# Attention, then experts, then an MLP on one core: the second attention tile's scores in other PSUM banks with idle products behind them, and loads issued three at a time

## The chip, the cores and the metric

The kernel runs on one core of a Trainium2 chip. The metric is the device time of one execution in microseconds (us). Engines: TensorE (PE) multiplies matrices, VectorE (DVE) and ScalarE (ACT) do elementwise work, GpSimd (POOL) builds constants and issues indirect transfers, SyncE (SP) issues nearly all other transfers. PSUM is the memory that PE writes to, in banks of 512 fp32 columns; SBUF is the main on-chip memory.

## What is computed

Three layers, one after the other, on 1152 tokens (2 sequences of 576) with 512 features:

```python
# attention, 8 heads of 64, each query sees the 64 positions up to its own
scores = where(0 <= i - j < 64, q @ k.T / 8, -1e9)
x = softmax(scores) @ v                       # (1152, 512)
# each token goes to one of 8 experts, at most 288 tokens each
e = argmax(x @ w_gate); g = softmax(x @ w_gate)[e]
x = g * (relu(x @ w1[e]) @ w2[e])             # zero for tokens over the capacity
# MLP with a per-feature negative slope
h = x @ w_in                                  # (1152, 2048)
out = (max(h, 0) + alpha * min(h, 0)) @ w_out
```

## The kernel before, in words

The program is one straight list of instructions per engine; their order on each engine is the order in which the Python code emits them, and an engine takes its next instruction only when the one ahead of it has been taken. Semaphores carry the dependencies.

**Attention** (to about 41 us) goes through nine tiles of 128 tokens (`for t in range(NTILE + 2)`, lines 880 to 915). A tile is two chunks of 64 queries; a chunk sees two chunks of keys. The steps of one tile are spread over three rounds of the loop:

- `pe_scores(t)` (399): 16 products, which show as 32 matmuls, into two banks `sc`, one for each `s` (the first and second head of a pair); `p` counts the four pairs. The banks come from a pool of two, so the next tile's scores wait until both are read.
- `peak(t)` (412): DVE adds the mask and takes the row maximum, one instruction pair for each of the eight heads in the order `HEADS` (410), which alternates between the banks. Between heads, `step` lets DVE do a piece of the routing of earlier tiles, from the seventh tile on.
- `softmax(t)` (424): eight exponentials on ACT, in the same order.
- `pe_turn(t-1)`, `put_turn(t-1)` (429, 436): eight transposes of the earlier tile's exponentials, first bank's four heads first, then one copy for each bank from PSUM (ACT; for the last tile's second bank DVE).
- `pe_values(t-1)` (442): products with the values into a PSUM tile `av` of two banks, of which there is one; `put_values` (451) scales them on DVE into `xr`.
- `pe_columns`, `put_columns`, `pe_logits`, `put_logits` of `t-2` (461 to 479): transpose, copy, and gate logits.

**Inputs.** SP issues all queries (`qT`), keys (`kT`) and values (`v`) at the start in the order of their use (lines 272 to 291), 256 to 384 KB each; POOL copies values into a second, shifted layout (`more_values`, 326). `keep_busy(6)` (300, 306) puts six bf16 products of 512 columns on PE ahead of the first scores; their results are not used.

**The star.** After the first four tiles' routing, `choose_star` (629) picks the expert with the most tokens so far. SP reads its number and loads that expert's weights: four chunks of 512 KB by `load` (100) and four by `load_star_w2` (694), the latter into the room of the first sequence's keys and queries. POOL scatters the tokens' rows `xr` to HBM (`scatter`, 763) from the same time on. `go_ahead` (730) multiplies the star's weights with its first tokens while the last tiles are routed: line 745 reads the first four chunks, line 756 the other four. The next weights (`load_on(star_rows())`, 941) wait for rows that are gathered after all scatters.

**Experts** (to about 209 us) and **MLP** (to the end) split each fp32 weight into a high and a low part (ACT and DVE) and make three products for one; the change doesn't touch them.

Of the kernel before, what the change touches and what calls it, by code (L numbers as in the profile page):

```python
# [7 lines left out]
F32 = mybir.dt.float32  # L8
# [19 lines left out]
def attention_moe_mlp_kernel(  # L28
# [13 lines left out]
    nc = tc.nc  # L42
# [41 lines left out]
    at_expert = {}  # L84

    def moe_chunk(n):
        p, c = stream[n]
        if p not in at_expert:
            at_expert[p] = nc.values_load(inci[0:1, NS + p:NS + p + 1], engines=(mybir.EngineType.SP,),
                                          min_val=0, max_val=n_moe - 8)  # L90
        return wmoe[bass.ds(at_expert[p] + c, 1)].rearrange("o p f -> (o p) f")
# [8 lines left out]
    def take(n):  # L100
        slot = next(x for x in free if fits(n, x))
        free.remove(slot)
        place[n] = slot
        return slot

    def load(n, after=None):
        pool, tag = take(n)
        raws[n] = pool.tile([128, 1024], F32, name="raw", tag=tag)
        if n < n_moe:
            ins = nc.sync.dma_start(raws[n], moe_chunk(n))  # L110
            if after is not None:
                tc.add_manual_dep(ins.ins, after.ins.name, mybir.DependencyInfo(
                    mybir.DependencyClass.Sync, mybir.DependencyReason.DATA), reason="rows first")
        else:
            nc.sync.dma_start(raws[n].bitcast(I32), wmlp[n - n_moe].bitcast(I32))

# [105 lines left out]
    with tc.manual_schedule():  # L222
# [13 lines left out]
        with ExitStack() as es:  # L236
# [6 lines left out]
            ps_s = es.enter_context(tc.tile_pool(name="ps_s", bufs=2, space=PSUM))  # L243
            ps_t = es.enter_context(tc.tile_pool(name="ps_t", bufs=2, space=PSUM))
            ps_a = es.enter_context(tc.tile_pool(name="ps_a", bufs=1, space=PSUM))
            ps_l = es.enter_context(tc.tile_pool(name="ps_l", bufs=1, space=PSUM))

            kT, qT = ([pool.tile([128, NCH, 4, 64], F32, name=n, tag=n) for pool in heads_p] for n in ("kT", "qT"))
# [6 lines left out]
            lgs = att.tile([128, NTILE, NE], F32, name="lgs")  # L255
            xr = att.tile([128, NTILE, ROW], F32, name="xr")

            def load_heads(b, c0, c1):
                for dst, src in ((qT, q), (kT, k)):
                    nc.sync.dma_start(dst[b][:, c0:c1], src[b, :, c0:c1])  # L260

            def values(b, w):
                return vv[b][w % 2][w // 4][:, w // 2 % 2, :VW]

            def load_v(b, j):

                dst, n = (values(b, 2 * j), 128) if j < 4 else (values(b, 7)[64:], 64)
                nc.sync.dma_start(dst, v[b, 128 * j:128 * j + n, :])

            z = att.tile([128, 128], F32, name="z")  # L270
            nc.vector.memset(z, 0.0)
# [28 lines left out]
            def keep_busy(n):  # L300
                ps = ps_l.tile([128, 512], F32, name="idle", tag="lg")
                for _ in range(n):
                    nc.tensor.matmul(ps, busy[:, :128], busy, start=True, stop=True)
# [83 lines left out]
            def step(n=1):  # L387
                for _ in range(n):
                    if chain:
                        next(chain[0], None)  # L390
# [5 lines left out]
            def chunks(t):  # L396
                return [divmod(2 * t + e, NCH) for e in range(2)]

            def pe_scores(t):
                sc = [ps_s.tile([128, 4, 128], F32, name="sc", tag="sc") for _ in range(2)]  # L400
                for p in range(4):
                    for s in range(2):
                        h = slice(64 * s, 64 * s + 64)
                        for e, (b, i) in enumerate(chunks(t)):
                            w = max(i - 1, 0)
                            nc.tensor.matmul(sc[s][64 * e:64 * e + 64, p, :], qT[b][h, i, p, :],  # L406
                                             kT[b][h, w:w + 2, p, :])
                scs[t] = sc

            HEADS = [(p, s) for p in range(4) for s in range(2)]  # L410

            def peak(t, steps):
                nms[t] = sm.tile([128, 2, 4], F32, name="nm", tag="nm")
                sc = scs[t]
                scs[t] = [wk.tile([128, 4, 128], F32, name="ms", tag="ms") for _ in range(2)]
                pts[t] = [wk.tile([128, 4, 128], F32, name="pt", tag="pt") for _ in range(2)]
                m = mk[tuple(i == 0 for _, i in chunks(t))]
                for p, s in HEADS:
                    nc.vector.tensor_tensor_reduce(
                        out=scs[t][s][:, p, :], in0=sc[s][:, p, :], in1=m, scale=-0.125, scalar=3e38,  # L420
                        op0=ALU.add, op1=ALU.min, accum_out=nms[t][:, s, p:p + 1])
                    step(steps)
# [206 lines left out]
            def choose_star():  # L629
                key = once("skey", NE)  # L630
                most, keyp = once("most", 1), once("skeyp", 1, dtype=I32)
                nc.vector.tensor_tensor(key, so_far, rev, op=ALU.add)
                yield
                nc.vector.tensor_reduce(most, key, axis=AX.X, op=ALU.max)
                yield
                nc.vector.tensor_scalar(keyp, most, 64.0, None, op0=ALU.mult)
                yield
                nc.vector.tensor_scalar(star[:, 0:1], keyp, 56, 56, op0=ALU.bitwise_and, op1=ALU.bitwise_xor)
                yield
                at_expert[0] = nc.values_load(star[0:1, 0:1], engines=(mybir.EngineType.SP,),  # L640
                                              min_val=0, max_val=n_moe - 8)
                for c in range(4):
                    load(c)
                for n in range(2):
                    load_star_w2(n)
                nc.vector.tensor_scalar(bias, key, most, MARK, op0=ALU.is_equal, op1=ALU.mult)
                yield
                nc.vector.tensor_tensor(bias, bias, rev, op=ALU.add)
                yield
                mine = once("mine0", NE)  # L650
                nc.vector.scalar_tensor_tensor(mine, bias, MARK, found[:, 2], op0=ALU.is_ge, op1=ALU.mult)
                yield
                nc.vector.tensor_reduce(seg[:, 0:1], mine, axis=AX.X, op=ALU.add)
                yield
# [39 lines left out]
            def load_star_w2(n):  # L694

                two = heads_p[0].tile([128, 4 * S], F32, name=f"sw{n}", tag=("kT", "qT")[n])
                for c in (2 * n, 2 * n + 1):
                    w = two[:, 1024 * (c % 2):1024 * (c % 2) + 1024]
                    nc.sync.dma_start(w, wmoe[bass.ds(at_expert[0] + (4 + c), 1)].rearrange("o p f -> (o p) f"))
                    star_w2.append(w.rearrange("p (k f) -> p k f", k=2))  # L700
                    if c < 3:
                        raws[4 + c] = w
# [68 lines left out]
            def once(name, *shape, dtype=F32):  # L771
                return sm.tile([128, *shape], dtype, name=name, tag=name, bufs=1)
# [107 lines left out]
            for t in range(NTILE + 2):  # L880
                if t < NTILE:
                    pe_scores(t)
                    peak(t, 1 + (t in (6, 7)))
                if 1 <= t <= NTILE:
                    pe_turn(t - 1)
                    put_turn(t - 1)
                if t == NTILE:
                    run(*chain)
                    choose(b1)
                if t >= 2:  # L890
                    pe_columns(t - 2)
                    put_columns(t - 2)
                if t < NTILE:
                    softmax(t, HEADS)
                if t == NTILE + 1:
                    pe_ahead((0,))
                    dispatch(b1)
                    while waiting:
                        scatter(*waiting.pop(0))
                if 1 <= t <= NTILE:  # L900
                    pe_values(t - 1)
                if t >= 2:
                    pe_logits(t - 2)
                if 1 <= t <= NTILE:
                    put_values(t - 1)
                if t >= 2:
                    put_logits(t - 2)
                if t == NTILE:
                    pe_dispatch(b1)
                    weigh(b1)  # L910
                pe_free.append(t)
                step(2)
                pe_free.clear()
                if t == 5:
                    chain.append(route(b0))
# [452 lines left out]
        with tc.If(n_over > 0, preferred_fallthrough_block=True):  # L1368
# [31 lines left out]
            for p in range(NE):  # L1400
# [5 lines left out]
                with tc.If(here > 0), ExitStack() as es:  # L1406
# [6 lines left out]
                    at = nc.values_load(inci[0:1, NS + p:NS + p + 1], engines=(mybir.EngineType.SP,),  # L1413
                                        min_val=0, max_val=n_moe - 8)
# [84 lines left out]
```

## Time and profile before

| | us |
|---|---|
| three timed runs | 417.22, 417.91, 415.33 |
| their median | 417.22 |
| the profiled execution, its own time | 418.03 |
| its span, first to last instruction | 416.3 |

The profile is of one execution. A chain of waits is followed back from the last instruction: at each step to what released it, or to the instruction before it on its engine. A timeline row has the start, the duration (of a merged group from its first start to its last end), engine, line, operation, tile written and read, and in brackets the idle time before it with what ended it. In windows, PEclk is the granted clock of PE, 1.00 for 2.4 GHz and 0.50 for 1.2 GHz, and the DMA share is that of 16 transfer engines.

### The profile page before, as it was taken

How to read it: one execution, taken by the hardware profiler on the slowest of the kernel's cores; microseconds unless marked ns; L12 is line 12 of the kernel's file. 1: busy time of each engine (PE TensorE's matmuls, PEld its weight loads, DVE VectorE, ACT ScalarE, POOL GpSimd, SP SyncE). 2: the span in 40 equal slices, each digit the busy share in tenths (PEclk: the TensorE clock that was granted, in tenths of full speed). 3: DMA queues.
4: the chain of work that ended last, by engine and by line, in shares of the span. 5: the costliest groups of instructions: out<-in, count | busy, mean ns of one | idle time of the engine just before them, and what ended most of it. 6: DMA issues, size and time to landing. Idle time of an engine off the chain costs nothing.

```text
span 416.3 us, 7856 instructions
## 1 busy us (share of the span) xinstructions
PE 396.3 (95%) x2925; PEld 351.4 (84%) x2925; DVE 285.4 (69%) x676; ACT 198.2 (48%) x371; POOL 58.2 (14%) x125
## 2 busy tenths in 40 slices
PE   6999789999999998999999999999999999999990
PEld 4888588789999876779999988998899988999880
DVE  2788567688997854536779966999949982356220
ACT  3788415567376453333457655676307720255000
POOL 4721236310000560000000000000000000000431
PEclk9999869999999999999999999999999999999997
DMA  7920953999988899731423243333411000000221
GB/s 265 371 59 8 351 231 129 333 411 401 313 290 284 248 306 323 272 97 46 153 86 118 101 153 112 142 111 141 140 64 54 0 2 0 0 2 1 78 101 56
DMA packets 20447, 66.13 MB, mean 159 GB/s; under 512 B 2992, under 2 KB 2992, under 8 KB 20400
## 3 DMA queue, kind: packets, MB, share of 16 engines
q1 hardware_dynamic: 17872, 58.00, 39.9%
q0 software_dynamic: 2528, 7.53, 5.0%
q8 instruction: 25, 0.41, 0.4%
q14 instruction: 22, 0.18, 0.1%
HBM read 60.74 MB, written 4.79 MB: 157 GB/s over the span
## 4 chain that ended last, share of the span: by engine, by line
PE 87%; DVE 5%; DMA 3%; ACT 2%; issue 2%; POOLq 0%; ACTq 0%; POOL 0%; DVEq 0%
PE gps L220 24%; PE ops L1326 24%; PE y L220 8%; PE hps L1033 6%; PE sps L220 3%; PE sy L220 3%; DMA raw<-moe_in 3%; PE sc L406 3%; PE av L448 2%; PE tp L434 2%; PE py L1205 2%; PE aps L745 2%; PE ay L756 2%; PE tx L464 1%; PE xap L689 1%
## 5 line engine op out<-in xcount | busy, mean ns | idle before, releaser
L144 DVE TENSOR_TENSOR wlo<-raw,whi 128x1024 fp32r<-128x1024 f32 x45 | 54.2, 1223 | 19.2 <-ACT whi L1017 13.7
L220 PE MATMUL gps<-x2h,wlo 128*128 128x384 f32 x192 | 64.2, 334 | 0.0
L220 PE MATMUL gps<-x2h,whi 128*128 128x384 f32 x192 | 64.2, 334 | 0.0
L220 PE MATMUL gps<-x2l,whi 128*128 128x384 f32 x192 | 64.2, 334 | 0.0
L1326 PE MATMUL ops<-whi,gl 128*128 128x512 f32 x144 | 56.1, 390 | 0.0
L1326 PE MATMUL ops<-wlo,gh 128*128 128x512 f32 x144 | 56.1, 390 | 0.0
L1326 PE MATMUL ops<-whi,gh 128*128 128x512 f32 x144 | 56.0, 389 | 0.0
L1302 ACT ACTIVATE u<-gps,one 128x384 f32<-128x384 f32 x48 | 27.7, 577 | 55.0 <-PE gps L220 55.0
L1334 POOL DMA_INDIRECT out<-acc,tok x9 | 8.7, 965 | 245.9 <-ACTq L1368 233.1
L1303 DVE SCALAR_TENSOR_TENSOR g<-gps,slope,u 128x384 f32<-128x384 f32 x48 | 29.4, 613 | 18.9 <-ACT u L1302 18.8
L1332 DVE SCALAR_TENSOR_TENSOR acc<-ops,gate,acc 128x512 f32<-128x512 f32 x27 | 19.9, 748 | 30.7 <-PE ops L1326 30.7
L1017 ACT CAST whi<-raw 128x1024 fp32r<-128x1024 f32 x30 | 31.0, 1049 | 16.6 <-PE y L220 11.9
L220 PEld LDWEIGHTS gps<-x2l,whi 128*128 128x128 f32 x192 | 36.0, 188 | 0.1
L220 PEld LDWEIGHTS gps<-x2h,whi 128*128 128x128 f32 x192 | 36.0, 188 | 0.1
L220 PEld LDWEIGHTS gps<-x2h,wlo 128*128 128x128 f32 x192 | 36.0, 188 | 0.0
L1313 ACT ACTIVATE gh<-g,sign 128x384 fp32r<-128x384 f32 x48 | 29.3, 611 | 9.5 <-DVE g L1303 9.5
L1326 PEld LDWEIGHTS ops<-whi,gl 128*128 128x128 f32 x144 | 27.0, 188 | 5.6
L1326 PEld LDWEIGHTS ops<-wlo,gh 128*128 128x128 f32 x144 | 27.0, 188 | 5.6
L1326 PEld LDWEIGHTS ops<-whi,gh 128*128 128x128 f32 x144 | 27.0, 188 | 5.5
L1314 DVE SCALAR_TENSOR_TENSOR gl<-g,sign,gh 128x384 fp32r<-128x384 f32 x48 | 29.2, 609 | 0.2 <-ACT gh L1313 0.2
L220 PE MATMUL y<-hh,whi 128*128 128x256 f32 x96 | 27.7, 288 | 1.6 <-ACT spht L1196 1.6
L190 DVE TENSOR_TENSOR wlo<-w,whi 128x512 fp32r<-128x512 f32 x32 | 21.9, 686 | 7.9 <-ACT whi L189 7.8
(267 smaller groups left out, 816.5 us busy)
## 6 DMA issues: line engine op xcount, KB each, us to landing
raw<-moe_in SPq DMA_DIRECT2D x61, 512.0 KB, 4.9
raw<-mlp_in SPq DMA_DIRECT2D x32, 512.0 KB, 3.3
v<-v_in SPq DMA_DIRECT2D x8, 260.0 KB
sw<-moe_in SPq DMA_DIRECT2D x4, 512.0 KB, 11.4
qT<-q_in SPq DMA_DIRECT2D x6, 256.0 KB
kT<-k_in SPq DMA_DIRECT2D x6, 256.0 KB, 5.9
qT<-q_in SPq DMA_DIRECT2D x2, 384.0 KB
kT<-k_in SPq DMA_DIRECT2D x2, 384.0 KB, 5.5
```

The costliest lines, as they stand in the source:

```text
L144: eng.tensor_tensor(lo, raws.pop(split[c]), hi.bitcast(F32), op=ALU.subtract)
L190: nc.vector.tensor_tensor(lo, w, hi.bitcast(F32), op=ALU.subtract)
L220: nc.tensor.matmul(ps, wa[i], xa[j], start=start and n == 0, stop=stop and n == 2)
L406: nc.tensor.matmul(sc[s][64 * e:64 * e + 64, p, :], qT[b][h, i, p, :], kT[b][h, w:w + 2, p, :])
L1017: (nc.vector.tensor_copy if c % 4 == 3 else nc.scalar.copy)(ring_tiles(c)[0], raws[split[c]])
L1033: nc.tensor.matmul(ps[:, f, :], (hi, lo)[i][:, kk, fs], xt[j][:, kk, :], start=n == kk == 0, stop=n == 2 and kk == 3)
L1302: nc.scalar.activation(out=u, in_=ps, func=AF.Copy, scale=one[:, ft:ft + 1])
L1303: nc.vector.scalar_tensor_tensor(g, ps, slope[:, ft:ft + 1], u, op0=ALU.mult, op1=ALU.max)
L1313: nc.scalar.activation(out=gh, in_=g, func=AF.Copy, scale=sg)
L1314: nc.vector.scalar_tensor_tensor(gl, g, sg, gh.bitcast(F32), op0=ALU.mult, op1=ALU.subtract)
L1326: nc.tensor.matmul(ps, a_[:, ts_], b_[:, f % 2, :], start=f == 0 and n == 0, stop=f == 3 and n == 2)
L1332: nc.vector.scalar_tensor_tensor(acc[:, tt, :], ps, sc, acc[:, tt, :], op0=ALU.mult, op1=ALU.add)
```

## The change

Five edits.

1. The scores of the second tile (`t == 1`) are written to a tile `sc1` in the place of `av`, the two banks that hold the values' products, instead of the two `sc` banks.
2. Behind the scores of the first tile PE gets four idle products, behind those of the second tile three.
3. `HEADS` goes through the four pairs of the first bank, then those of the second.
4. Input transfers are counted in `paced`. From the ninth on each waits until the one three places ahead of it has landed. The first keys are issued on ACT's queue instead of SP's. The gate weights and `alpha` are not counted.
5. The star's eight weight loads are counted anew; from the fourth on each waits until the one three places ahead has landed.

```diff
 def load(n, after=None):
...
+            return ins
...
+            inputs = []
+            def paced(ins, n=8):
+                inputs.append(ins)
+                if len(inputs) > n:
+                    tc.add_manual_dep(ins.ins, inputs[-4].ins.name, mybir.DependencyInfo(
+                        mybir.DependencyClass.Sync, mybir.DependencyReason.DATA), reason="three at a time")
             def load_heads(b, c0, c1):
-                for dst, src in ((qT, q), (kT, k)):
-                    nc.sync.dma_start(dst[b][:, c0:c1], src[b, :, c0:c1])
+                for dst, src, queue in ((qT, q, nc.sync), (kT, k, nc.sync if b or c0 else nc.scalar)):
+                    paced(queue.dma_start(dst[b][:, c0:c1], src[b, :, c0:c1]))
...
             def load_v(b, j):
-                nc.sync.dma_start(dst, v[b, 128 * j:128 * j + n, :])
+                paced(nc.sync.dma_start(dst, v[b, 128 * j:128 * j + n, :]))
...
             def pe_scores(t):
-                sc = [ps_s.tile([128, 4, 128], F32, name="sc", tag="sc") for _ in range(2)]
+                if t == 1:
+                    both = ps_a.tile([128, 2, 512], F32, name="sc1", tag="av")
+                    sc = [both[:, s].rearrange("q (p k) -> q p k", k=128) for s in range(2)]
+                else:
+                    sc = [ps_s.tile([128, 4, 128], F32, name="sc", tag="sc") for _ in range(2)]
...
-            HEADS = [(p, s) for p in range(4) for s in range(2)]
+            HEADS = [(p, s) for s in range(2) for p in range(4)]
...
             def choose_star():
+                inputs.clear()
                 for c in range(4):
-                    load(c)
+                    paced(load(c), 3)
...
             def load_star_w2(n):
-                    nc.sync.dma_start(w, wmoe[bass.ds(at_expert[0] + (4 + c), 1)].rearrange("o p f -> (o p) f"))
+                    paced(nc.sync.dma_start(w, wmoe[bass.ds(at_expert[0] + (4 + c), 1)].rearrange("o p f -> (o p) f")), 3)
...
             for t in range(NTILE + 2):
                 if t < NTILE:
                     pe_scores(t)
+                    if t < 2:
+                        keep_busy(4 - t)
                     peak(t, 1 + (t in (6, 7)))
```

## Rows read from the trace of the kernel before

**Rows 1.** Page: PE's busy time and share; its clock in 40 slices.
```profile
PE 396.3 (95%) x2925; PEld 351.4 (84%) x2925; DVE 285.4 (69%) x676; ACT 198.2 (48%) x371; POOL 58.2 (14%) x125
...
PEclk9999869999999999999999999999999999999997
```

**Rows 2.** Chain of waits, first 20 us: start, us, what.
```profile
1.71 2.74 PE idle L303 x6
4.45 1.99 PE sc L406 x32
...
8.20 2.23 PE sc L406 x30
10.42 1.90 PE tp L434 x8
12.32 1.93 PE av L448 x32
14.25 1.03 PE sc L406 x32
...
16.75 1.08 PE av L448 x32
...
18.50 1.03 PE sc L406 x32
```

**Rows 3.** Timeline, first two tiles: exponentials, second scores, a copy.
```profile
6.86 2.44 ACT L426 ACTIVATE pt<-ms,nm 128x128 f32<-128x128 f32 x8 [4.56 <-DVE nm L419]
...
8.20 2.23 PE L406 MATMUL sc<-kT,qT 64*64 64x128 f32 x32 [1.83 <-DVE nm L419]
...
11.50 0.59 ACT L440 COPY ptT<-tp 128x512 f32<-128x512 f32 x1 [2.19 <-PE tp L434]
```

**Rows 4.** Windows: length, busy time of each engine, PEclk, DMA share, GB/s.
```profile
0.00:6.45 6.45, 4.66 (x38) 2.32 (x38) 0.79 (x4) 1.49 (x2) 2.46 (x12) 1.00 0.65 200
6.45:8.20 1.75, 0.01 (x1) 0.04 (x1) 1.68 (x15) 1.34 (x5) 0.57 (x2) 1.00 1.04 354
8.20:14.20 6.00, 6.00 (x75) 5.22 (x76) 1.88 (x18) 3.54 (x11) 5.41 (x40) 1.00 1.04 369
14.20:18.45 4.25, 4.21 (x97) 3.72 (x95) 3.95 (x23) 3.62 (x12) 2.94 (x9) 1.00 1.04 383
```

**Rows 5.** Issues of keys: count, size of one, median us to landing.
```profile
kT<-k_in SPq DMA_DIRECT2D x6, 256.0 KB, 5.9
```

**Rows 6.** Chain of waits, 40 to 64 us: start, us, what.
```profile
44.07 1.74 PE tx L464
...
47.40 2.04 ACT pt L426 x7
...
49.48 1.33 PE tp L434 x5
50.81 0.85 PE tx L464 x4
...
57.71 0.96 PE lg L474 x16
```

**Rows 7.** Timeline, ninth tile: VectorE and ScalarE after their waits.
```profile
45.75 0.29 DVE L419 CUSTOM_DVE_ANT_0 ms<-sc,mf 128x128 f32<-128x128 f32 x1 [3.15 <-PE tx L464]
45.83 1.07 ACT L440 COPY ptT<-tp 128x512 f32<-128x512 f32 x2 [4.43 <-PE tx L464]
```

**Rows 8.** Window of the lower granted clock, columns as in rows 4.
```profile
48.30:58.60 10.30, 9.76 (x93) 8.49 (x93) 6.01 (x35) 3.29 (x9) 1.11 (x3) 0.50 0.76 307
```

**Rows 9.** Transfer queues from 43 to 45 us: packets, MB, share.
```profile
q1 hardware_dynamic: 128, 0.46, 85.5%
```

**Rows 10.** Timeline and SP's waits: star's first loads, its first product, SP's next load.
```profile
41.22 2.42 SPq L110 DMA_DIRECT2D raw<-moe_in  x4
...
62.97 5.34 PE L745 MATMUL aps<-raw,axT 128*128 128x256 f32 x24
...
SPq L110 <- DMA sx<-xe,ixe: 24.1, 1, 24.1
```

## What is predicted, before the changed kernel is built or run

> **What bounds the kernel now.** I read the page first [rows 1]: TensorE (PE) is busy for 396.3 us, 95% of the span, so time can only be won where PE is idle, where it runs at the lower of its clock levels, or where it does work that can go. The row of slices shows the granted clock low in one place, in the slices after 40 us. Then I read the chain of waits of the first 20 us [rows 2] and of 40 to 60 us [rows 6]: the only two stretches that the edits touch.
>
> In the first stretch the reader is to see two things. The chain leaves PE once: the second tile's scores (8.20) wait for the last of eight peaks on VectorE (DVE), since both score banks are still being read; the timeline gives that wait as 1.83 us [rows 3]. And before 14.2 us everything on PE takes about twice as long as later: 32 score matmuls take 1.99 and 2.23 us, later 1.03; the values 1.93, then 1.08; the transposes in between took 1.90 [rows 2]. An idle product of 512 columns takes 2.74/6 = 0.46 us, which is the 1.2 GHz level. The column of granted clock reads 1.00 in these stretches [rows 4], so here I go by durations. PE worked from 1.71 to 6.44, was idle until 8.20, worked on without a gap, and was at 2.4 GHz from 14.2 on.
>
> In the second stretch one transpose stands in the chain for 1.74 us [rows 6], and VectorE and ScalarE (ACT) both wait for PE: 3.15 and 4.43 us that end at 45.8 [rows 7]. Afterwards the granted clock is 0.50 for 10.3 us [rows 8].
>
> The tiles between go at 4.25 us each with PE busy for 4.21 of them and VectorE for 3.95 [rows 4]. A lead won before them is carried through, as long as the inputs keep up.
>
> **The change, part by part.**
>
> 1. *Second tile's scores in the values' banks.* They no longer wait for the first tile's peaks: the 1.83 us go. In their place PE runs four idle products, then the scores, then three idle products. The values of the first tile now wait until the second tile's peaks have read those banks.
>
> When the clock rises with the gap filled I can't read anywhere, so I bound it. Earliest: everything from 6.45 on at 2.4 GHz. Four products 4 x 0.23 = 0.92 (half of the 0.46), scores 1.1 to 8.5, three products to 9.2. ACT's eight exponentials of the first tile end at 6.86 + 2.44 = 9.30 [rows 3], so the turn ends at 9.9 or so; two copies of 0.59 [rows 3], the values (1.1, half of them beside the second copy) end at 11.5. They end at 14.25 now [rows 2]: 2.7 won. Latest: the clock rises at 14.2 as now. Four products 1.83, scores 2.1, three products 1.37, turn 1.97, values 2.0: the values end near 15.7, 1.5 lost. Middle: it rises during the four products. They end at 7.8, the scores at 8.9, three products at 9.6, turn at 10.65, copies at 11.4, values at 12.0: 2.2 won. The second tile's peaks (1.76 us for eight, as now from 6.44 to 8.20, and from 8.9 on) end at 10.7, before the values want the banks at 10.9; that new wait is hidden by 0.2 us, and in the earliest case it is the limit. I take the middle, because PE then works without the 1.75 us of idleness that stood in its first 14 us.
>
> What is late next: VectorE. Between a tile's values and its logits it scales the values, takes the peaks of a later tile and copies the columns, nearly all of its 3.95 us for a tile [rows 4]. From 12.0 that gives logits at 15.85; they take 0.65 (from 16.75 + 1.08 to 18.50 [rows 2]), so the fourth tile's scores stand at 16.5, against 18.5 now. So **2.0 us** of the 2.2 are carried on; bounds 2.6 won and 1.5 lost.
>
> 2. *Order of heads.* Eight exponentials in the order of the banks instead of alternating. In the steady tiles PE reaches the turn after the exponentials are over, so nothing changes. For the last tile the chain shows five transposes behind the exponentials, 1.33 us, then the columns and the values [rows 6]. The seventh exponential ends at 49.44, the eighth near 49.75. With the first bank's four heads done halfway, one transpose is left behind the eighth, and the columns start at 50.1 instead of 50.8: 0.7 at the lower clock, half of that at the upper. I take **0.6**; bounds 0 (the bank's copy on ACT takes the place) and 0.9.
>
> 3. *Input transfers three at a time, from the ninth on; the first keys on ACT's queue.* The keys' issue now stands at the head of ACT's queue, whose first exponential is at 6.86 [rows 3]: hidden. The first scores start behind the idle products, so earlier keys win nothing. With the pacing, SP waits; behind it on its queue are only more inputs and, at 41 us, the star's weights. The cost is bandwidth. Now a key transfer of 256 KB takes 5.9 us from issue to landing [rows 5] at 383 GB/s [rows 4]: 2.26 MB, or 8.6 transfers, under way. What three give is not in the trace. Upper bound: the same 383 GB/s. Lower: in proportion, 3/8.6 of it, 134 GB/s. What is needed: the first eight transfers (2.1 MB) land near 8.6 (1.29 MB by 6.45, 0.62 more by 8.20 [rows 4]); then 2.24 MB more must be there for the fifth tile's scores at 18.5 + 4.25 - 2.0 = 20.7, that is 185 GB/s. In the first 6.45 us, in which transfers start one by one and the wait for the first bytes is included, 200 GB/s were moved [rows 4]. I take 300, between that row and the upper end, and the cost **0**.
>
> The Trainium skill (DMA: Bandwidth & Descriptors, "Anatomy of one DMA — SWDGE (gpsimd) path") gives a fixed 2.0 us beside the bytes at 436 GB/s, though for the other descriptor path. By that, an estimate: 256 KB take 2.6 us alone, and three under way move 0.30 MB per us. That is slower than the row but over the need, and it leaves the sum as it is.
>
> 4. *Star's weights three at a time.* The eight loads of 512 KB are issued from 41.22 on; the first product that reads them is at 62.97, and SP then waits 24.1 us for the star's gathered rows before its next load [rows 10]. All eight in the 21.7 us up to that product would be 193 GB/s, half of the 383 of rows 4, and the last four are wanted later still: hidden, cost 0. The weights that follow start when the star's rows are gathered, so I let their stream shift with the lead. Is there a gain? The stall at 42 to 46 lies exactly where loads and row scatters meet: in 43 to 45 us the load queue alone moved packets, 128 of them [rows 9]. If the deep load queue makes this stall, pacing shortens it. But VectorE's wait begins at 42.6 [rows 7], when at most three loads have been issued (four in 2.42 us from 41.22 [rows 10]), and three would still be under way. I take **0**; bounds: nothing, and 2.1 us of idleness plus the lower clock. The latter's worth: six PE pieces of the chain, from the transposes at 49.48 (1.33) to the logits at 57.71 (0.96), sum to 7.9 us at 0.50 [rows 6, 8]; at full clock about half, 3.7 us less.
>
> The Trainium skill (DMA: Bandwidth & Descriptors, "Queues, rings and completion order") says that each DMA engine goes round robin between the queues it has work for. By that rule a deep load queue could not hold the scatters back, pacing would change nothing here, and the first rival below would fall away. Rows 9, with one queue moving alone, show no such even sharing.
>
> Sum: 2.0 + 0.6 = 2.6 us. The profiled execution took 418.03 us, its span is 416.3, and the median of three runs is 417.22 (415.33 to 417.91): 0.8 lower, within their spread. 418.03 - 2.6 = 415.4 for an execution like it; 417.22 - 2.6 = **414.6** for the median.
>
> **Rivals.**
> - *The stall shrinks too.* For: its place, and that the load queue alone moves then. Against: it begins before a fourth load is issued. It would give the 2.6 plus 1.5 (some of the idleness) to 5.8 (all of it and the clock): 413.1 to 408.8, middle 410.5.
> - *The clock rises late.* Then the seven products lie on PE's path at 0.46 each and the first stretch loses 1.5 while the order of heads still wins 0.6: 417.22 + 0.9 = 418.1. For: 1.71 to 6.44 brought no rise. Against: the gap that followed is just what goes.
> - *Three transfers starve the attention (slower).* Place: the scores of the fifth tile and later. It decides from 185 GB/s downward. At 134 GB/s the remaining 5.0 MB last 37 us from 8.6, so the last tile's keys land at 46, where the loads of the star begin at 41.2 now, right beside that tile's scores: 4.7 later, 422. At 155 GB/s they land at 41: the gain is just eaten. Against: the 300 taken above. I put 420 on it.
>
> **How the numbers follow.** Forecast as summed 0.48; stall shrinks 0.27; late clock 0.13; starved 0.12. The forecast's own range is 413.5 to 416. With 418.5 at the top the late clock is in and only the starved runs are out; at the bottom 409 leaves out only the very best of the second case. One per cent, 4.2 us, is about what a measurement of this kernel tells from no change: faster by more (under 413.05) is 0.25 of the stall case and 0.09 of the forecast's early edge, 0.34; slower by more (over 421.4) is half of the starved case, 0.06; the rest, 0.60, is within it.
>
> **What would show it.** Right: in the changed profile the second tile's scores start near 7.8 without a wait on VectorE and last about 1.1; values of the first tile end near 12; the fourth tile's scores stand near 16.5; one transpose behind the last exponential; scores that wait for no input; star's first product about 2.6 us earlier than 62.97, with everything behind it shifted alike. Wrong: scores of 2 us after 8 us (late clock); scores waiting for a key transfer (starved); VectorE and ACT not waiting at the eighth tile, or no granted clock of 0.50 (the stall was the load queue's). If the lead is there at 17 us and gone at 170, it is lost in the weights' stream, and my claim that this shifts with the star's rows is the wrong step.

## The result: 413.51 us after, 417.37 before

20 runs of each kernel: before 417.37 us (414.86 to 418.89), after 413.51 (410.46 to 418.07), ratio 0.9911 [0.9892, 0.993]. That is 3.9 us less, 0.9%; the interval reaches from 2.9 to 4.5 us. The forecast was 414.6, the range 409.0 to 418.5. The profiled execution of after took 413.85 us, 4.2 less than that of before, and its span is 412.1, also 4.2 less. Here and below, ratios and intervals are taken from the fast runs of both kernels and are not the quotients of the medians beside them.

The page of after, lines that answer to [rows 1]:
```profile
PE 392.2 (95%) x2932; PEld 347.3 (84%) x2932; DVE 285.2 (69%) x676; ACT 198.2 (48%) x371; POOL 57.2 (14%) x125
...
PEclk9999899999999999999999999999999999999997
```
PE is busy for 4.1 us less though it has seven more instructions, and the fifth slice, which holds 41 to 51 us, reads 8 where before had 8 and 6 in two slices.

The timeline of after, first two tiles and then the ninth (start, duration, engine, line, operation, tiles, idle before), answering to [rows 3, 7, 10]. Line 420 is the scores, 313 the idle products, 448 the transposes, 462 the values, 433 the peaks, 454 the copies, 760 the star:
```profile
4.86 1.99 PE L420 MATMUL sc<-kT,qT 64*64 64x128 f32 x32 [0.41 <-DMA kT<-k_in]
6.77 1.14 PE L313 MATMUL idle<-ahead_y 128*128 128x512 bf16 x4
...
7.84 1.10 PE L420 MATMUL sc<-kT,qT 64*64 64x128 f32 x32
...
10.82 0.08 DVE L433 DVE_READ_ACCUMULATOR2_ANT nm<- 128x1 f32 x1
...
11.16 1.15 PE L462 MATMUL av<-v,ptT 128*64 128x65 f32 x32 [0.58 <-POOL back L360]
...
43.73 0.29 DVE L433 CUSTOM_DVE_ANT_0 ms<-sc,mf 128x128 f32<-128x128 f32 x1 [3.00 <-remote]
43.81 1.07 ACT L454 COPY ptT<-tp 128x512 f32<-128x512 f32 x2 [4.29 <-remote]
44.45 1.94 PE L462 MATMUL av<-v,ptT 128*64 128x65 f32 x32 [2.67 <-ACT ptT L454]
...
57.99 1.03 PE L760 MATMUL aps<-raw,axT 128*128 128x256 f32 x4
...
59.94 4.58 PE L760 MATMUL aps<-raw,axT 128*128 128x256 f32 x20 [0.93 <-issue]
```
The reader is to see three things. The second tile's scores start at 7.84 with no wait and take 1.10 where they took 2.23 from 8.20: the wait of [rows 3] is gone, and PE is on its upper level from about 7.0, when the four products (1.14 for four) speed up, instead of 14.2. (That part is not the edit alone: in all twelve profiles of the experiments below, two of them without edits 1 and 2, the clock first rose between 4.6 and 7.6 us. The profile of before is the only one in which it took until 14.2. The trace's record of the granted clock begins with the first rise; ahead of it the PEclk column of [rows 4] reads 1.00 without a record.) The values start at 11.16, 0.26 after the last peak of the second tile has ended at 10.90; the releaser in the brackets is inferred. (In a kernel of the third group that POOL instruction comes later than the values, and the values again start 0.26 after the last peak; in five kernels the profile names the last peak itself.) So the new wait on the banks is real, and is the last to end. At the ninth tile nothing has changed: VectorE and ScalarE still wait for 3.00 and 4.29 us, and PE for 2.67.

The chain of waits of after, first 20 us, then the last tile's turn, answering to [rows 2, 6]:
```profile
11.17 1.14 PE av L462 x32
...
15.92 0.64 PE lg L488 x16
16.56 1.03 PE sc L420 x32
...
46.39 0.76 PE lg L488 x16
47.15 1.45 PE tp L448 x8
```
The fourth tile's scores stand at 16.56, before at 18.50 [rows 2]: 1.94 us won between these two executions. How much of it is the late rise of the clock in the one of before is taken up below. The last tile's transposes (47.15) follow the logits at once, where five of them came behind the exponentials before [rows 6].

Windows of after, columns as in [rows 4]; the first two answer to those rows, the last two to [rows 8]:
```profile
8.20:14.20 6.00, 5.42 (x111) 4.48 (x104) 4.13 (x32) 5.22 (x17) 5.49 (x39) 1.00 0.74 246
14.20:18.45 4.25, 4.21 (x94) 3.71 (x93) 3.51 (x24) 3.41 (x11) 1.47 (x5) 1.00 0.86 286
44.45:47.98 3.53, 3.53 (x52) 3.51 (x53) 3.15 (x21) 3.25 (x10) 0.00 (x0) 0.52 1.03 390
47.98:52.00 4.02, 3.53 (x68) 3.14 (x67) 3.06 (x15) 1.28 (x3) 0.00 (x0) 1.00 0.89 348
```
With three transfers under way 246 to 286 GB/s are moved, where 369 and 383 were before, and nothing on PE waits for an input after the first scores. The low granted clock lasts 3.5 us here, 10.3 before [rows 8].

The ninth tile's values in the kernel before (timeline), for the line at 44.45 above:
```profile
46.47 1.17 PE L448 MATMUL av<-v,ptT 128*64 128x65 f32 x32 [2.13 <-ACT ptT L440]
```
Where the 4.2 us of the profiled pair come from: 1.94 at the fourth tile's scores; 2.0 at the ninth tile's values (44.45, before 46.47); 5.0 at the star's first product (57.99, before 62.97 [rows 10]), the extra 3.0 mainly, by its length, from the shorter stretch at the lower clock. Behind that product the changed kernel waits 0.93 us, which the kernel before did not, and 4.2 are left at the end. What this wait is was not found.

So far this reads like the prediction's step 1 with some luck. The experiments say otherwise.

### The profile page after: what moved, and what is told of

Its sections match the earlier page's. It is cut to its first block, busy times and chain, and to the rows that moved or that the text cites. A ratio compares the mean times of both kernels' runs of the same rounds, so it can differ in the third digit from the quotient of the medians.

```text
span 412.1 us, 7881 instructions
## 1 busy us (share of the span) xinstructions
PE 392.2 (95%) x2932; PEld 347.3 (84%) x2932; DVE 285.2 (69%) x676; ACT 198.2 (48%) x371; POOL 57.2 (14%) x125
## 4 chain that ended last, share of the span: by engine, by line
PE 84%; DMA 4%; DVE 3%; ACT 2%; issue 2%; another core or an unknown queue 1%; POOL 1%; SPq 0%; POOLq 0%; ACTq 0%
PE gps L221 24%; PE ops L1343 24%; PE y L221 8%; PE hps L1050 6%; PE sps L221 3%; PE sy L221 3%; DMA raw<-moe_in 3%; PE av L462 2%; PE py L1222 2%; PE aps L760 2%; PE ay L771 2%; PE sc L420 2%; PE tp L448 1%; DVE wlo L145 1%; DMA v<-v_in 1%
```

## The experiments

Kernels ran in three groups of four, each group on one chip beside the kernel before: 418.25 us (35 runs), 410.19 (28) and 417.06 (31). The chips differ by 2%, so ratios are compared, inside a group first; the changed kernel itself ran only in the third group and in the first comparison. Where the expectations use letters, A is the prediction's account, in which the pacing is worth nothing, and C the one on packets of instructions that is formed below.

### First group: are the parts worth what the prediction gave them?

**The change without pacing.** No transfer waits, and the first keys are on SP's queue again.
```diff
-                if len(inputs) > n:
+                if False:
-                for dst, src, queue in ((qT, q, nc.sync), (kT, k, nc.sync if b or c0 else nc.scalar)):
+                for dst, src, queue in ((qT, q, nc.sync), (kT, k, nc.sync)):
```


> The change without its transfers' pacing: all inputs and star loads issued as before, keys on SP's queue. Left in: scores of the second tile in the values' banks, idle products, order of heads. If pacing is worth nothing (theory A): the same as the whole change, 3.9 us below the kernel before, within 0.7; first scores back at 4.4 instead of 4.86. If pacing brings the part of the gain that the prediction didn't count (theory B): 2.6 us below before or less, so at least 1.3 slower than the whole change. The low clock after 44 us: under A its length varies as it likes, under B it is longer than the 3.4 us of the change.

Measured: 418.83 us, ratio 0.9994 [0.9956, 1.0032]. No gain is left. The front is as in the changed kernel (values at 11.20), and then PE stops twice with nothing in the profile that it waits for. Timeline of this kernel:
```profile
16.53 0.54 PE L420 MATMUL sc<-kT,qT 64*64 64x128 f32 x9
18.34 0.88 PE L420 MATMUL sc<-kT,qT 64*64 64x128 f32 x23 [1.27 <-issue]
...
24.33 0.27 PE L478 MATMUL tx<-identf,xr 128*128 128x128 f32 x1
25.59 0.55 PE L478 MATMUL tx<-identf,xr 128*128 128x128 f32 x3 [0.99 <-issue]
```
The stops lie inside a run of equal products, 9 into the fourth tile's scores and, a round later, 1 into the third tile's transposes for the gate: 1.27 + 0.99 = 2.26 us, which eats the lead of 1.9 to 2.0.

**Only the pacing.** The kernel before with both pacings and the first keys on ACT's queue; scores, products and order of heads are those of before.
```diff
-                if t == 1:
-                    both = ps_a.tile([128, 2, 512], F32, name="sc1", tag="av")
...
-            HEADS = [(p, s) for s in range(2) for p in range(4)]
+            HEADS = [(p, s) for p in range(4) for s in range(2)]
...
-                    if t < 2:
-                        keep_busy(4 - t)
```


> The kernel before with the pacing alone, and the first keys on ACT's queue. Theory A: no change, within 0.7 us, or 0.4 slower because the first keys land later. Theory B: 1.3 us or more below the kernel before, with a shorter stall at 42 to 46 us or a shorter stretch at the low clock. The fifth tile's scores wait for no input in either.

Measured: 417.33 us, ratio 0.9974 [0.9945, 1.0003]: between 2.3 us won and 0.1 lost, so neither nothing, as the prediction had it, nor 1.3 us is excluded. PE doesn't stop, and this execution had something to lose. The front is that of before, but PE's clock first rose at 5.73, fell at 9.15 behind the wait for the peaks and rose again at 12.56, where before it rose at 14.19. So this execution has a lead without edits 1 and 2, and keeps it. Chain of waits, fourth and sixth tile's scores, then the sixth tile's of before (the fourth tile's stand at 18.50 [rows 2]):
```profile
17.44 1.03 PE sc L416 x32
...
25.98 1.03 PE sc L416 x32
```
```profile
27.04 1.03 PE sc L406 x32
```
1.06 us ahead at both places.

**Banks and products alone** (edits 1 and 2): as the first kernel, and `HEADS` in the order of before.
```diff
-            HEADS = [(p, s) for s in range(2) for p in range(4)]
+            HEADS = [(p, s) for p in range(4) for s in range(2)]
```


> The kernel before with the second tile's scores in the values' banks and the idle products, nothing else. Prediction's step: 2.0 us below before; the fourth tile's scores near 16.1 to 16.5 instead of 18.5. A rival (the clock's share): 3 us or more below before, because the clock's low stretch after 44 us is shorter or gone as well.

Measured: 419.88 us, ratio 1.0020 [0.9989, 1.0051]. Its front was the best of the group (values at 10.15, fourth tile's scores at 15.56), and its stops the longest. Timeline:
```profile
16.89 0.88 PE L420 MATMUL sc<-kT,qT 64*64 64x128 f32 x23 [0.87 <-issue]
...
25.86 0.59 PE L478 MATMUL tx<-identf,xr 128*128 128x128 f32 x2 [2.60 <-issue]
```
The lead was 2.9 us (15.56 against 18.50 [rows 2]); the product that PE makes at 25.86 here, the kernel before has behind it by 25.18, as its timeline further down shows. The lead is more than gone.

**The order of heads alone** (edit 3): one line in the kernel before.
```diff
-            HEADS = [(p, s) for p in range(4) for s in range(2)]
+            HEADS = [(p, s) for s in range(2) for p in range(4)]
```


> The kernel before with the new order of heads alone. Prediction's step: 0.6 us below before, one or two transposes instead of five behind the last exponential. Rival: 0, since the copies that follow are no earlier. With so small a number the interval may take in both; the chain then decides.

Measured: 418.29 us, ratio 0.9998 [0.9975, 1.0022]. Nothing that can be told. By chance this profiled execution shows what the lead needs: PE's clock rose early without any edit for it, the fourth tile's scores stood at 16.95, and PE stopped twice. Windows (the first rise, the stretch behind the wait for the peaks), chain of waits, timeline:
```profile
5.19:8.60 3.41, 1.76 (x52) 1.34 (x46) 1.78 (x16) 2.23 (x8) 0.42 (x2) 1.00 1.00 346
8.60:12.01 3.41, 3.41 (x39) 2.75 (x31) 1.78 (x16) 1.52 (x4) 2.94 (x9) 0.50 1.03 399
```
```profile
16.95 0.59 PE sc L406 x14
...
27.65 1.03 PE sc L406 x32
```
```profile
18.55 0.81 PE L406 MATMUL sc<-kT,qT 64*64 64x128 f32 x18 [1.00 <-issue]
...
26.08 1.09 PE L448 MATMUL av<-v,ptT 128*64 128x65 f32 x29 [0.89 <-issue]
```
Of a lead of 1.55 us (16.95 against 18.50) nothing is left at the sixth tile's scores: 27.65, 0.6 behind the kernel before, where the paced kernel was 1.06 ahead. With seven idle products fewer ahead of them, both stops lie five products later in the program. They belong to a place in PE's list of instructions, not to a tile, a transfer of data or a time.

**What follows.** No part by itself shows a gain that can be told from none, and together they are worth 0.5 to 0.9%, so they don't simply add: the lead is lost in unpaced kernels at two places of PE's program. The windows from the start to the first stop, and from there to the second, count the products and weight loads in between (columns as in [rows 4]: PE, then the weight loads):
```profile
0.00:17.07 17.07, 14.69 (x217) 9.82 (x218) 8.82 (x60) 10.40 (x30) 10.40 (x57) 1.00 0.91 296
17.07:24.60 7.53, 6.23 (x124) 5.33 (x124) 4.58 (x32) 4.26 (x14) 4.50 (x13) 1.00 0.87 283
```
435 instructions, then 248. The page of after lists, among the transfer queues, one of the kind "instruction":
```profile
q8 instruction: 25, 0.41, 0.4%
```
25 packets of 0.41/25 MB = 16 KB each; PE's 2932 products and 2932 weight loads are 235 for a packet, close to the 248 (not every instruction of PE leaves a record). I read it so that the queue carries PE's program, in blocks of some 250 instructions, and the two stops are the ends of blocks. Theory C, of which the line of transfers is argued and not seen: the next block comes late because its packet goes through the same 16 transfer engines behind the many input transfers. The transfer view of the unpaced change, 23 to 24 us, and of the change, 17.5 to 18.5, has one such packet each:
```profile
q8 instruction: 1, 0.02, 6.9%
```
```profile
q8 instruction: 1, 0.02, 6.5%
```
It starts at 23.25 unpaced, and PE goes on at 25.59; at 17.71 in the change, where PE wants that block only at 22.8. The windows of the unpaced kernel say when it came (last two columns: transfer share, GB/s):
```profile
22.00:23.00 1.00, 1.00 (x40) 0.98 (x40) 0.95 (x3) 1.00 (x5) 0.01 (x1) 1.00 0.93 256
23.00:24.00 1.00, 1.00 (x25) 0.83 (x15) 0.38 (x4) 0.26 (x1) 0.40 (x2) 1.00 0.39 122
```
It came when the inputs ran out. It does so in each of the five kernels whose inputs are unpaced (the kernel before among them): that packet starts between 22.9 and 23.6, and PE is past its end of block at 25.5 to 26.1 (in the kernel before at about 25.3). This is a gate that stands at 25 to 26 us however early PE comes there (23.3 to 25.3).

And why doesn't the kernel before stop? It arrives just as the gate opens. Its block ends five products later, like that of the order of heads, two products into the fourth tile's values. Timeline of before:
```profile
25.18 1.29 PE L448 MATMUL av<-v,ptT 128*64 128x65 f32 x32
```
Those values took 1.29 us, elsewhere 1.15: 0.14 us is all that shows. A lead of 2 us against it is a stop of 2 us, here or at the first gate.

### Second group: which pacing, and do the keys matter?

**Only the inputs paced.** The star's loads are issued as before.
```diff
-                    paced(load(c), 3)
+                    load(c)
...
-                    paced(nc.sync.dma_start(w, ...), 3)
+                    nc.sync.dma_start(w, ...)
```


> The whole change, but the star's eight loads issued as before, without pacing; the inputs stay paced. Theory C: without pacing PE's next block of instructions comes to the core behind eight input transfers, so a PE that is two us ahead arrives before its instructions; pacing the inputs is what keeps the lead. Under C this kernel keeps the whole gain, 3 to 4.5 us below before, with no wait of 0.8 us or more on PE between 12 and 30 us. Rival D: the star's pacing is what matters (the stall at the ninth tile or the low clock behind it): then it is within 1.5 us of before.

Measured: 407.63 us against 410.19, ratio 0.9945 [0.9927, 0.9963]: 2.3 us (1.5 to 3.0), less than the 3 to 4.5 expected. PE's timeline has no stop at either place:
```profile
15.59 1.10 PE L420 MATMUL sc<-kT,qT 64*64 64x128 f32 x32
...
21.80 0.60 PE L478 MATMUL tx<-identf,xr 128*128 128x128 f32 x4
```

**Only the star paced**, the inputs unpaced and the first keys on SP.
```diff
-                if len(inputs) > n:
+                if n < 8 and len(inputs) > n:
-                for dst, src, queue in ((qT, q, nc.sync), (kT, k, nc.sync if b or c0 else nc.scalar)):
+                for dst, src, queue in ((qT, q, nc.sync), (kT, k, nc.sync)):
```


> The whole change, but inputs issued as before (keys on SP's queue); only the star's loads are paced. Theory C: no better than the kernel without any pacing, within 1 us of before, with two waits of about one us or more on PE between 15 and 27 us that nothing in the profile releases. Rival D: 2.5 us or more below before.

Measured: 410.82 us, ratio 1.0008 [0.9990, 1.0026]. The stops are back, at the same 9 and 1 products (timeline), and a window behind the second shows what it costs besides:
```profile
17.20 0.88 PE L420 MATMUL sc<-kT,qT 64*64 64x128 f32 x23 [1.13 <-issue]
...
25.55 0.66 PE L478 MATMUL tx<-identf,xr 128*128 128x128 f32 x3 [2.09 <-issue]
```
```profile
25.85:32.68 6.83, 6.83 (x92) 6.20 (x91) 3.55 (x21) 1.09 (x3) 0.00 (x0) 0.50 0.01 2
```
PE idled 2.09 us and was then granted 0.50 for 6.8 us. The banks kernel of the first group, with its stop of 2.60, had the same (0.50 for 6.7 us from 25.86) in its profiled execution; that this is why it came out at 1.0020 with the best front of the group is likely, but not shown.

**The first keys on SP's queue**, all else as changed.
```diff
-                for dst, src, queue in ((qT, q, nc.sync), (kT, k, nc.sync if b or c0 else nc.scalar)):
+                for dst, src, queue in ((qT, q, nc.sync), (kT, k, nc.sync)):
```


> The whole change with the first keys issued on SP's queue as before. In the profile of the change the first scores waited 0.41 us for those keys. If the second queue makes them late, the first scores start at 4.4 and the kernel is up to 0.4 us faster than the change; if the transfers' sharing does it, the start stays at 4.8 and the time is the change's.

Measured: 407.65 us, ratio 0.9938 [0.9915, 0.9960], no different from the inputs-only kernel above, which has them on ACT (and the star unpaced). This kernel and the one before it (star paced, keys on SP) differ in the inputs' pacing alone, on one chip: 407.65 against 410.82, 3.2 us by the medians, with intervals well apart. That is what the inputs' pacing is worth to a kernel that has the lead. But the timeline has the first scores earlier:
```profile
4.38 1.76 PE L420 MATMUL sc<-kT,qT 64*64 64x128 f32 x32
```
4.38 and no wait, where the change has 4.86 behind a wait of 0.41 for the keys. ACT's queue brings them later, not earlier; here nothing that can be measured follows from it.

**Twelve idle products behind the ninth tile's columns**, meant to keep PE busy in the stall there; they compute nothing that is used.
```diff
+                    if t == NTILE - 1:
+                        keep_busy(12)
                     put_columns(t - 2)
```


> The whole change with twelve idle products behind the ninth tile's columns (2.6 us at the upper clock), where PE stood 2.67 us. If that idleness brings the low clock after it, there is no granted clock of 0.50 between 40 and 60 us and the kernel is 0.8 (the change's 3.4 us stretch) to 3 us faster than the change. If the low clock has another cause, or the products delay the values, it is the same or up to 1 us slower.

Measured: 409.88 us, ratio 0.9990 [0.9964, 1.0016], 2.2 us slower than the two kernels with paced inputs above. On this chip there is no stall at the ninth tile, in any of the four kernels profiled, nor a granted clock under 1.00 from 40 to 60 us in the ones with paced inputs. The products just lie on the path (2.75 us), and the question of the stall stays open.

### Third group: how deep may the queue be, and does the change repeat?

**The change itself, again**, on a chip whose four profiles have the stall; no edit.

> The changed kernel once more, as the mate of the three others on one chip. By the study so far 2.5 to 4 us below the kernel before; 2.5 where PE has no stall at the ninth tile, more where it has.

Measured: 415.82 us against 417.06, ratio 0.9950 [0.9916, 0.9984]: 2.1 us by the ratio (0.7 to 3.5), 1.2 by the medians; less than the 3.9 at first and less than the expected 2.5, though the stall is there. The two intervals overlap from 0.9916 to 0.9930.

**Only the inputs paced, again** (the diff of the second group).

> The whole change without the pacing of the star's loads. Theory C (the pacing of the inputs is all that matters): within 0.6 us of the changed kernel. Rival D (the star's pacing adds something of its own): 0.8 us or more slower than it.

Measured: 414.53 us, ratio 0.9940 [0.9906, 0.9974]. The star's pacing adds nothing on this chip either, though the stall is there (PE idle for 2.74 us, with the pacing 0.38 and 2.12 in two pieces).

**All seven idle products behind the second tile's scores.**
```diff
-                    if t < 2:
-                        keep_busy(4 - t)
+                    if t == 1:
+                        keep_busy(7)
```


> The changed kernel with all seven idle products behind the second tile's scores, none behind the first's. In the change the second tile's peaks waited for its scores behind four products, and the first values waited for the last of those peaks. Without the four, the peaks follow those of the first tile at once and the first values stand 0.4 us earlier: up to 0.4 us faster than the changed kernel. If the clock rises later for it, or the copies on ACT become the limit, the same time.

Measured: 414.96 us, ratio 0.9941 [0.9913, 0.9968], as the others. The second tile's scores come four products earlier, but the last peak doesn't: in the changed kernel's profile of this group it ends at 10.29 and the values start at 10.55. Timeline:
```profile
10.15 0.08 DVE L433 DVE_READ_ACCUMULATOR2_ANT nm<- 128x1 f32 x1
...
10.49 1.15 PE L462 MATMUL av<-v,ptT 128*64 128x65 f32 x32 [0.53 <-POOL v L344]
```
VectorE goes through sixteen peaks without a break, the last ends at 10.23, and the values start 0.26 behind it: here VectorE is the limit of this stretch.

**Five transfers under way instead of three** (inputs; the star stays at three).
```diff
-                    tc.add_manual_dep(ins.ins, inputs[-4].ins.name, mybir.DependencyInfo(
+                    tc.add_manual_dep(ins.ins, inputs[-6 if n == 8 else -4].ins.name, mybir.DependencyInfo(
```


> The changed kernel with five input transfers under way instead of three. Theory C: PE's block of instructions comes later than with three (0.8 us after it is asked for there, 4.4 to 6.5 with eight), at some 2 to 3.5 us, still ahead of PE, which needs 7 us for a block of 248 products and loads: no wait of its own at 436 or 684, same time as the changed kernel within 0.6 us. If such waits are back, the time is 1 to 2.5 us longer.

Measured: 414.22 us, ratio 0.9937 [0.9903, 0.9972], again as the others. But against the expectation the second stop is back, at the product at which the unpaced kernels stop. Timeline:
```profile
22.42 0.27 PE L478 MATMUL tx<-identf,xr 128*128 128x128 f32 x1
23.42 0.55 PE L478 MATMUL tx<-identf,xr 128*128 128x128 f32 x3 [0.73 <-issue]
```
The packet starts at 21.10 here: at 17.7 with three under way, 21.1 with five, 22.9 to 23.6 with all. The stop of 0.73 us cost no time that these runs resolve (in this execution no low clock followed, neither there nor behind the 2.12 us for which PE stood at the ninth tile).

## Why the prediction was right, and where it was not

**Bound and step 1, right in place; the size is partly luck.** Forecast: second scores near 7.8, 1.1 long; fourth tile's scores at 16.5; 2.0 us. Measured: 7.84, 1.10; 16.56; 1.94. Errors in it cancel. The values ended at 12.31, not 12.0, because the wait on the banks that I called hidden by 0.2 us is the one that ends last: the last peak ended at 10.90, not 10.7, and PE started another 0.26 behind it, a term that the prediction doesn't have. What made up for it is VectorE: from the end of those values to the logits 3.61 us passed (12.31 to 15.92), not the forecast 3.85.

And the yardstick, 18.50, comes from one execution, whose clock rose at 14.19. The two other profiles with the front of before have these scores at 17.44 and 16.95. Where the clock first rose at nearly the same time and the first keys came on ACT's queue in both, edits 1 to 3 are worth 1.5 us at this place (17.44 in the pacing-only kernel, 5.73; 15.95 in the changed kernel of the third group, 5.69). In these two profiles with the old front the clock fell again behind the wait for the peaks; in no profile with the new front did it fall there. So the edit's place is shown, and its size lies somewhere between 0.4 us (16.56 against 16.95) and 3, by when the clock rises in the two executions compared.

**Step 2, in time not settled.** Alone the order gives 0.9998 [0.9975, 1.0022], between 1.0 us won and 0.9 lost: the forecast 0.6 is neither shown nor excluded. The chains say on what it depends. From the eighth tile's values to the last tile's columns 4.34 us pass before (46.47 to 50.81) and in the pacing-only kernel; with the new order, in the unpaced change, 3.78 (47.17 to 50.95), so 0.56 less:
```profile
47.17 1.17 PE av L462 x32
...
48.89 2.06 PE tp L448 x8
50.95 0.85 PE tx L478 x4
```
In these three the values run at the upper clock. Where the low stretch begins before them (values of 2.0 us), it is 4.66 with the old order (banks and products alone) as with the new (order alone, and the change of the third group): PE comes to the transposes later, and the exponentials are off the chain in either order. So the exponentials' absence from the chain of after doesn't show the edit at work.

**Step 3 is the one that failed.** "I take 300, between that row and the upper end, and the cost **0**", and "earlier keys win nothing". The rate was near what was taken (286 GB/s at 14 to 18 us, 185 needed), the cost was nothing, and still the step was wrong, since it asked only what pacing costs: without the inputs' pacing the other edits are worth nothing (0.9994 and 1.0008), with it 3.2 us more on the same chip. The total came out in its range because the edit that was counted as worth 0 was part of the change. I had written that a lead won in front "is carried through, as long as the inputs keep up": it is carried through as long as PE's own program keeps up, for which the prediction has no term. It was to be read in the trace of before: its instruction queue has a packet at 23.06, when the inputs run dry, and the values behind the next end of block took 1.29 us. The keys came later instead of earlier, which cost 0.4 us at the start and nothing after.

**Step 4, right.** The star's pacing is worth nothing that can be measured (0.9940 without, 0.9950 with it on one chip).

**The rivals.** The stall did not shrink: 2.67 us of PE idleness, as before (0.42 and 2.13 in two pieces). (For this rival 413.1 to 408.8 was given with a middle of 410.5; their middle is 411.0.) What shrank in the profiled pair is the low clock behind it, by its length most of the extra 3.0 us, and nothing says that this is the pacing's doing. Windows of the unpaced change and of the pacing alone, both of the first group:
```profile
52.00:56.00 4.00, 3.33 (x73) 3.12 (x73) 3.25 (x20) 1.28 (x3) 0.00 (x0) 1.00 1.02 417
```
```profile
52.00:56.00 4.00, 3.67 (x43) 3.58 (x40) 3.06 (x21) 0.59 (x1) 0.00 (x0) 0.50 0.83 260
```
The unpaced kernel has the short stretch, the paced one the long, and the changed kernel itself had 3.4 us in the first comparison and 6.8 in the third group. What sets the length was not found. The late clock didn't come (7.0 us), and no scores starved.

**The size.** 2.6 was forecast; 3.9, 2.1 and (inputs paced, on the chip without the stall) 0.55% of 410.19 = 2.3 us were measured. I read this as a lead of some 2 us that the paced kernels keep, and in the first comparison a part of the low clock besides. That the lead is lost without pacing and kept with it is shown; its share of the total, and how the rest is made up, is argued. The changed kernel and the pacing alone never ran side by side, so what edits 1 to 3 add to the pacing is not measured in time.

**Open.** Why results of PE reach VectorE and ScalarE 3 to 4 us late at the ninth tile in every profile but the four of the second group's chip; loads behind the scatters, or the scatters behind the loads, were not tried.

## What to carry to other kernels

An engine's program is input, too: where a kernel issues all its loads at once, look for the packets of the instruction queues, and for stops marked "issue" inside a run of equal instructions, before a lead is counted as won. Edits that show nothing each by itself can be worth something together, so undo a part of the whole change as well as trying each part alone. Ask of a step not only what it costs but what the others would be without it. And a lead read between two profiles holds the clock's course in both: compare when it rose in each.

## What the runs showed of the hardware that had not been expected

- PE takes its program in blocks of some 250 recorded instructions, 16 KB in a packet. PE goes on 2.3 to 2.7 us after such a packet starts (23.25 and 25.59, 23.43 and 25.86, 22.89 and 25.55, 23.57 and 26.08, 21.10 and 23.42).
- In the kernels that stop, the block before that one shows the same distance: 15.70 and 18.34, 14.57 and 16.89, 14.76 and 17.20, 15.96 and 18.55.
- The packet for the second of these blocks starts 4.9 to 6.5 us after PE has gone on with the first in the kernels that stop with all inputs queued (18.34 and 23.25, 16.89 and 23.43), and comes when they run out. The Trainium skill (DMA: Bandwidth & Descriptors, "Queues, rings and completion order") says that an engine takes turns between the queues it has work for, packet by packet. By that rule a lone packet would not have to wait for the others to run dry. These runs don't agree, unless the packet was asked for late: the profile shows when it moves, not when it was wanted.
- Stops of 2.1 and 2.6 us of PE near 25 us were followed by 6.8 and 6.7 us at a granted clock of 0.50, shorter ones (0.73 to 1.3) by none in these executions. The length of the stop alone doesn't decide: with five transfers under way PE stood 2.12 us at the ninth tile, and the clock stayed at 1.00.
- PE's clock first rose at 4.6 to 7.6 us in thirteen profiles and at 14.19 in that of before, though up to the end of the first scores PE's instructions are the same in all of them.
- The same kernel took 410.19 us on one chip, 418.25 and 417.06 on two others and 417.37 in the first comparison. The four kernels profiled on the chip with the short time don't have the stall at the ninth tile; the kernel before was not profiled there.
